# A small input tile moved into the norm constant's place, in a one-core S4D and token-mixer kernel

## The chip, the cores and the metric

The kernel runs on one core of a Trainium2 chip. Its time is the device time of one launch in microseconds (us). The time that is compared is the median of several runs; the profile is of one execution.

A core has a matrix engine (PE, whose weight loads are listed apart as PEld), a vector engine (DVE), a scalar engine (ACT), a general engine (POOL), and a queue (SP) from which nearly all transfers are issued. On-chip memory (SBUF) has 128 partitions; a tile takes the same bytes, at the same place, in each of its partitions.

## What is computed

A block of 2048 tokens by 448 channels goes through two parts, each with a layer norm whose shift, scale and gate come from a conditioning vector `c`:

```python
mod = (_silu(c) @ w_mod).reshape(c.shape[0], 6, 1, -1)
sa, ca, ga, sb, cb, gb = (mod[:, 0], ..., mod[:, 5])
h = _layernorm(x) * (1 + ca) + sa
x = x + ga * _A_ref(h, ...)          # S4D: a long convolution along the tokens
h = _layernorm(x) * (1 + cb) + sb
x = x + gb * _B_ref(h, ...)          # mixer: an MLP along the tokens
```

`_A_ref` builds a convolution kernel of 2048 taps for each of 448 channels out of 256 complex exponentials, and convolves by Fourier transforms of length 4096. `_B_ref` normalizes once more, multiplies by `w1` (2048 to 1792, along the tokens), adds `b1`, takes GELU, multiplies by `w2` (1792 to 2048) and adds `b2`. All is float32.

## The kernel before, in words

**Stages.** The first 56 steps make the convolution kernel, 8 channels at a step: ACT takes exponentials and sines, POOL and DVE multiply them (L656, L679 to L687), PE sums them up (L710). Between them run the first norm, the transform of the input (L553, L581) and, from step 32 on, the products of spectra and the inverse transform for the first half of the channels (L805, L814, L816, L817, L831, L837). After step 56 come the second half of the channels, the return to tokens (L1243 to L1259) and the second norm (`ln_mod`, `ln_out`). The token MLP then has two products. Each is done as three products of a high and a low part: L1373 to L1375 for `w1`, with the normalized tokens `h3h` and `h3l` as the streamed operand, and L1442 to L1444 for `w2`, with `uh` and `ul`. A weight tile is 128 by 896; it is loaded into `w`, and ACT and DVE split it into `whi` (L207) and `wlo` (L216).

**Order.** The order on PE, ACT, DVE and POOL is the one in which the code issues. SP's order is written out by hand at the beginning, up to step 8, and again from the second half of the channels to the end of the first MLP product's normalized rows; between the two the framework's planner orders the transfers.

**Places in SBUF.** Tiles come from pools. A pool takes its place on a stack from below, or, with `side="right"`, on a second stack from above. The pool `cp` is the first of the lower stack and stays to the end. It holds `mod3` to `mod5`, then `eps_t`, `sc`, `ft`, `b1` and `b2`. All other pools of the lower stack lie above it: `y0` (`wm0` and `yk0`, the spectra of the first half), `qp`, `sp2`, `xp` (`xt`, `yt`), `up` (`yi`, `uo`), `fp` (`yk1`, `u`, `si`, `zx`, `zy`, `z`, `vt`), `swp`, and in the MLP `mk` (`h3h`, `h3l`), `mu` (`uh`, `ul`) and `m2r` (`u`, `x2`, `y`). On the upper stack are, among others, the tables `tab`, the exponents' tiles, `mag`, `w` of POOL's products, `E` and `G`, and in the MLP the weights `w`, `whi`, `wlo` (pool `mw`), the rows `xt` that the second norm adds to (pool `mx`) and the pool `mr` of the second norm.

Each tile's bytes are rounded up to a multiple of 32. In the program before, `eps_t` lies at byte 21888 of each partition, `sc` at 21920, `ft` at 21984, `wm0`, `yk0` and later `h3h` at 22368, `h3l` at 51040, `uh` at 79712 and `ul` at 92256.

**The two tiles.** `eps_t` (128 x 1) holds the norm's 1e-5. DVE writes it at L241; ACT reads it at L462 (first norm) and L1230 (second norm, 32 times); at L1332 ACT takes its square root in place, only to have a table loaded, and DVE writes it again at L1333. `sc` is four of the sixteen columns of a 112 x 16 tile: ACT writes exp(-c) there (L913), DVE turns it into silu(c) (L848 to L850) and spreads it out (L851, L508, L509) as the stationary operand of the products with `w_mod`.

Of the kernel before, what the change touches and what calls it, by code (L numbers as in the profile page):

```python
# [11 lines left out]
F32 = mybir.dt.float32  # L12
# [10 lines left out]
P = 128  # L23
# [198 lines left out]
def tile_adaln_s4d_mixer(ctx, tc, i, out):  # L222
# [10 lines left out]

    cp = ctx.enter_context(tc.tile_pool(name="cp", bufs=1))
    mod = [None] * 3 + [cp.tile([P, D], F32, name=f"mod{k}") for k in range(3, 6)]
    eps_t = cp.tile([P, 1], F32, name="eps_t")
    sc = cp.tile([112, 16], F32, name="sc")[:, 0:4]
    ft = cp.tile([P, 64], F32, name="ft")
    b1 = cp.tile([P, 14], F32, name="b1")
    b2 = cp.tile([P, 16], F32, name="b2")  # L240
# [1235 lines left out]
```

## Time and profile before

| | |
|---|---|
| median of 3 runs | 691.31 us (689.89 to 692.56) |
| the profiled execution's own time | 689.93 us |
| its span, first to last instruction | 688.0 us |
| mean granted PE clock in it | 0.969 |

A busy PE is not PE at its peak: matmuls overlap, so the pace is read from the starts of successive matmuls. A row of the groups by line gives line, engine, operation, tiles, shapes and count, then busy time and mean duration, then the engine's idle time just before and who ended it. A row of one tile's or one line's instructions gives a duration as least, median and largest in ns, and the start of the first and the last. A row of the stretches gives the length, then the busy time of each engine with its number of instructions, the granted PE clock, the share of time in which the DMA engines were busy, and what they moved in GB/s.

The span in 40 slices, from the page (one digit is the busy share in tenths, PEclk the granted PE clock):

```profile
PE   0887889879988899999999899999999999999997
PEld 0454445435545566565667667779999999999996
DVE  7599799888779596877967478777322543333331
ACT  5967698888989999999935588877222422222210
POOL 6497467358368888898847000000000000000000
PEclk9998979989999999999999999999999999999999
DMA  7695643568895956353359899946764255555530
```

Slice 1 is 17.2 us long, as all are. POOL's work ends in slice 22, with the convolution; the MLP fills slices 24 to 40.

### The profile page before, as it was taken

The page shows a single profiled execution, that of the slowest core. Times are in us where ns is not written, and L with a number is a line of the kernel's source. Part 1 is how long each engine was busy: PE and PEld are TensorE (multiplying, and loading weights), DVE is VectorE, ACT ScalarE, POOL GpSimd, SP SyncE. Part 2 cuts the span into 40 slices and gives each one's busy share as a digit, 9 for nine tenths or more (in the row PEclk, how much of TensorE's full clock was granted, in tenths as well). Part 3 has the DMA queues.
Part 4 walks back from the last instruction along what each step waited for, and adds up shares of the span by engine and source line. Part 5 has one row for each costly group of instructions (what it writes and reads, how often), then busy time and mean ns, then how long its engine had stood idle before and what let it go on. Part 6 is the DMA issues. An engine that isn't in the chain of part 4 may idle for free. (4 is left out here: it accounts for less than half of the span.)

```text
span 688.0 us, 18263 instructions
## 1 busy us (share of the span) xinstructions
PE 622.3 (90%) x7180; PEld 458.4 (67%) x7180; DVE 452.8 (66%) x870; ACT 438.8 (64%) x880; POOL 268.6 (39%) x323
## 2 busy tenths in 40 slices
PE   0887889879988899999999899999999999999997
PEld 0454445435545566565667667779999999999996
DVE  7599799888779596877967478777322543333331
ACT  5967698888989999999935588877222422222210
POOL 6497467358368888898847000000000000000000
PEclk9998979989999999999999999999999999999999
DMA  7695643568895956353359899946764255555530
GB/s 175 198 196 129 204 161 120 185 212 260 249 298 175 239 134 195 97 152 101 107 158 321 227 251 242 239 123 175 194 190 136 84 163 160 162 161 162 161 114 28
DMA packets 105923, 121.14 MB, mean 176 GB/s; under 512 B 13098, under 2 KB 94286, under 8 KB 105710
## 3 DMA queue, kind: packets, MB, share of 16 engines
q1 hardware_dynamic: 104478, 113.92, 58.1%
q0 software_dynamic: 1360, 6.06, 4.0%
q8 instruction: 57, 0.93, 0.6%
q14 instruction: 28, 0.23, 0.1%
HBM read 84.59 MB, written 34.87 MB: 174 GB/s over the span
## 5 line engine op out<-in xcount | busy, mean ns | idle before, releaser
L207 ACT CAST whi<-w 128x896 fp32r<-128x896 f32 x64 | 59.9, 940 | 139.4 <-PE o L1443 87.1
L679 POOL TENSOR_TENSOR G<-mag,gs 128x512 f32<-128x512 f32 x56 | 71.8, 1282 | 67.4 <-ACT gs L675 67.2
L216 DVE TENSOR_TENSOR wlo<-w,whi 128x896 fp32r<-128x896 f32 x64 | 68.0, 1086 | 41.5 <-ACT whi L207 32.0
L1373 PE MATMUL acc<-h3h,whi 128*128 128x448 f32 x224 | 84.1, 375 | 1.3 <-ACT h3h L1278 1.3
L1374 PE MATMUL acc<-h3l,whi 128*128 128x448 f32 x224 | 82.8, 370 | 0.1
L1375 PE MATMUL acc<-h3h,wlo 128*128 128x448 f32 x224 | 82.4, 368 | 0.0
L1443 PE MATMUL o<-ul,whi 128*128 128x448 f32 x224 | 82.0, 366 | 0.0
L1444 PE MATMUL o<-uh,wlo 128*128 128x448 f32 x224 | 82.0, 366 | 0.0
L1442 PE MATMUL o<-uh,whi 128*128 128x448 f32 x224 | 82.0, 366 | 0.0
L710 PEld LDWEIGHTS kg<-E,G 128*32 128x32 f32 x3584 | 57.4, 116 | 35.5 <-issue 13.9
L627 PE MATMUL xg<-tab,lph 64*128 64x512 f32 x112 | 65.8, 589 | 11.2 <-ACT gs L676 4.6
L710 PE MATMUL kg<-E,G 128*32 128x64 f32 x3584 | 67.3, 230 | 7.8 <-ACT ks L724 3.4
L680 POOL TENSOR_TENSOR G<-mag,gs 128x512 f32<-128x512 f32 x56 | 72.0, 1285 | 0.0
L627 PE MATMUL xe<-tab,lph 64*128 64x512 f32 x112 | 65.8, 589 | 4.4 <-ACT gs L676 2.6
L1446 DVE SCALAR_TENSOR_TENSOR y<-o,b,mod 128x448 f32<-128x448 f32 x16 | 10.9, 684 | 83.1 <-PE o L1444 83.1
L656 POOL TENSOR_TENSOR m<-mag,w 128x512 f32<-128x512 f32 x56 | 59.0, 1054 | 4.4
L681 DVE TENSOR_TENSOR E<-m,xe 128x512 f32<-128x512 f32 x56 | 38.2, 682 | 22.9 <-ACT xe L674 19.1
L1373 PEld LDWEIGHTS acc<-h3h,whi 128*128 128x128 f32 x224 | 42.4, 189 | 14.6 <-ACT h L1283 4.2
L627 PE MATMUL xe<-tab,lex 64*128 64x512 f32 x56 | 31.2, 573 | 18.4 <-POOL dsk L477 17.1
L1374 PEld LDWEIGHTS acc<-h3l,whi 128*128 128x128 f32 x224 | 42.5, 190 | 4.2 <-DVE h3l L1285 0.4
L1375 PEld LDWEIGHTS acc<-h3h,wlo 128*128 128x128 f32 x224 | 42.5, 190 | 3.6
L1443 PEld LDWEIGHTS o<-ul,whi 128*128 128x128 f32 x224 | 42.1, 188 | 3.6
(239 smaller groups left out, 1445.7 us busy)
## 6 DMA issues: line engine op xcount, KB each, us to landing
w<-in_B_w_dram SPq DMA_DIRECT2D x64, 224.0 KB
w<-in_B_w_dram SPq DMA_DIRECT2D x32, 448.0 KB
yu_d<-yt SPq DMA_DIRECT2D x16, 448.0 KB
yi<-yu_d SPq DMA_DIRECT2D x16, 448.0 KB
us_d<-uo SPq DMA_DIRECT2D x16, 448.0 KB
u<-us_d SPq DMA_DIRECT2D x32, 224.0 KB
v_d<-vt SPq DMA_DIRECT2D x32, 224.0 KB
vt<-v_d SPq DMA_DIRECT2D x14, 448.0 KB
```

Source lines behind the costliest of these rows:

```text
L207: self.nc.scalar.copy(hi, w)
L216: eng.tensor_tensor(lo, w, hi.bitcast(F32), ALU.subtract)
L627: T.matmul(out[k], lhs[r], rhs[r], start=start, stop=stop)
L679: G.tensor_tensor(Gt[:, 1], mg_, v32(sg), ALU.mult)
L680: G.tensor_tensor(Gt[:, 0], mg_, v32(cg_), ALU.mult)
L710: T.matmul(kgs[g][32 * q : 32 * q + 32, m], Gt[:, c, d], E[:, c, d], start=h == 0 and c == 0 and m == 0, stop=h == 1 and c == 1, skip_grou ...
L1373: nc.tensor.matmul(acc[f], hi[:, fs], h3h[:, r], start=r == 0, stop=False)
L1374: nc.tensor.matmul(acc[f], hi[:, fs], h3l[:, r], start=False, stop=False)
L1375: nc.tensor.matmul(acc[f], lo[:, fs], h3h[:, r], start=False, stop=r == 15)
L1442: nc.tensor.matmul(o, hi[:, ks], uh[kh][:, k], start=kh == 0 and k == 0, stop=False)
L1443: nc.tensor.matmul(o, hi[:, ks], ul[kh][:, k], start=False, stop=False)
L1444: nc.tensor.matmul(o, lo[:, ks], uh[kh][:, k], start=False, stop=kh == 1 and k == 6)
```

## The change

`eps_t` and `sc` become two parts of one tile of 128 x 5: columns 0 to 3 (partitions 0 to 111) are `sc`, column 4 is `eps_t`. The padding of `sc` from 4 to 16 columns goes. Every later tile on the lower stack starts 64 bytes lower; nothing else is edited.

```diff
     mod = [None] * 3 + [cp.tile([P, D], F32, name=f"mod{k}") for k in range(3, 6)]
-    eps_t = cp.tile([P, 1], F32, name="eps_t")
-    sc = cp.tile([112, 16], F32, name="sc")[:, 0:4]
+    small_t = cp.tile([P, 5], F32, name="small_t")
+    eps_t, sc = small_t[:, 4:5], small_t[0:112, 0:4]
     ft = cp.tile([P, 64], F32, name="ft")
     b1 = cp.tile([P, 14], F32, name="b1")
     b2 = cp.tile([P, 16], F32, name="b2")
```

## The prediction

> **What bounds the kernel now.** I read the stretches first, because the change moves tiles in all stages and each stage has its own limit.
>
> ```profile
> core 0: us, PE busy (x) PEld busy (x) DVE busy (x) ACT busy (x) POOL busy (x), PEclk, DMA share, GB/s
> 150.00:200.00 50.00, 46.84 (x770) 24.36 (x769) 37.81 (x72) 43.50 (x89) 31.49 (x35) 0.96 0.81 243
> 200.00:250.00 50.00, 43.55 (x992) 27.03 (x987) 41.39 (x77) 46.79 (x92) 41.69 (x47) 1.00 0.74 211
> 350.00:370.00 20.00, 19.76 (x207) 13.79 (x197) 13.66 (x24) 9.17 (x39) 11.45 (x20) 1.00 0.83 241
> 370.00:385.00 15.00, 14.34 (x120) 11.06 (x120) 7.51 (x15) 8.67 (x31) 7.03 (x12) 1.00 0.94 301
> 385.00:402.00 17.00, 14.77 (x65) 9.79 (x63) 12.51 (x37) 10.75 (x25) 0.00 (x0) 0.90 0.86 225
> 402.00:465.00 63.00, 63.00 (x296) 48.22 (x295) 49.82 (x149) 51.11 (x113) 0.00 (x0) 1.00 0.89 206
> 465.00:546.00 81.00, 81.00 (x399) 74.58 (x398) 31.92 (x47) 28.70 (x38) 0.00 (x0) 1.00 0.57 165
> 546.00:684.00 138.00, 137.38 (x674) 126.14 (x672) 54.28 (x70) 29.47 (x33) 0.00 (x0) 1.00 0.48 137
> ```
>
> From 402 to 684 us PE never stops: this is the MLP, 282 us or 41% of the 688.0 us span, and it goes at PE's pace. In the earlier stages PE, ACT and POOL are all near full and share the limit. Between 350 and 402 the transfers are densest (0.83 to 0.94 of the DMA engines' time), and there PE stands still for 0.24 + 0.66 + 2.23 = 3.1 us. The list of waits agrees for the MLP: the long ones are waits for PE.
>
> ```profile
> ACT whi L207 <- PE o L1443: 87.1, 27, 3.3
> DVE y L1446 <- PE o L1444: 83.1, 16, 7.2
> ...
> PE xe L627 <- POOL dsk L477: 17.1, 1, 17.1
> ```
>
> The third is PE's wait at the very start, for the first loads and what is made of them.
>
> So a move of tiles can do much only if it alters how fast PE reads its operands; on other engines and on transfers it has a few us at stake at most.
>
> **The change part by part.** *(a) Two tiles become one.* No instruction, no operand size and no transfer is added or taken away. What could come in is a wait, if the order of accesses were kept for the whole tile instead of its two parts. The accesses:
>
> ```profile
> L913 ACT ACTIVATE sc<-cvec x1: 188/188/188, 14.1 to 14.1; 112x4 f32<-112x4 f32 x1
> L850 DVE TENSOR_TENSOR sc<-sc,cvec x1: 161/161/161, 18.2 to 18.2; 112x4 f32<-112x4 f32 x1
> L509 DVE COPY yk<-sc x1: 216/216/216, 239.7 to 239.7; 112x128 f32<-112x128 f32 x1
> ```
>
> ```profile
> L241 DVE MEMSET eps_t<- x1: 59/59/59, 0.8 to 0.8; 128x1 f32 x1
> L462 ACT ACTIVATE rs<-mv,eps_t x1: 308/308/308, 68.2 to 68.2; 128x16 f32<-128x16 f32 x1
> L1332 ACT ACTIVATE eps_t<-eps_t x1: 203/203/203, 384.4 to 384.4; 128x1 f32<-128x1 f32 x1
> ```
>
> In time the two tiles interleave as L241 (0.8 us), L913 (14.1), L850 (18.2), L462 (68.2), L509 (239.7), L1332 (384.4). Each new wait would be for something that ended 13, 50 or 144 us before: L913 for L241, L462 for L850, L1332 for L509. Nothing is late, so nothing queued behind these instructions on ACT is held. What a wait that is already met may still cost is an instruction of its own:
>
> ```profile
> L590 ACTq EVENT_SEMAPHORE  x8: 38/38/38, 162.0 to 207.5; - x8
> ```
>
> Three of 38 ns are 0.1 us. I take 0, and keep 0 to +0.1.
>
> *(b) 64 bytes.* With places in steps of 32 bytes, `eps_t` (4 bytes) and `sc` (64) take 32 + 64 = 96; the new tile (20 bytes) takes 32; the difference is 64, as the change says. A new wait by place needs a lower-stack tile that now touches a tile of the upper stack which it did not touch. Going through the places of all tiles of the program before, one pair does: the buffer of `yt` that starts at byte 120736, where a late buffer of POOL's `m2` ends; after the change they share 64 bytes. The last `yt` store is issued at 138.0 us, and the late `m2` buffers come into use after step 32, around 239 us.
>
> ```profile
> L558 SPq DMA_DIRECT2D yu_d<-yt x16: 512/530/594, 73.3 to 138.0; - x16
> ```
>
> A hundred us lie between; cost 0. All tiles of the lower stack move together and keep their places relative to one another.
>
> *(c) Reading and writing at a new place.* In the MLP the weights `w`, `whi`, `wlo` and the residual rows are on the upper stack and stay; the streamed operands move. `h3h` goes from byte 22368 to 22304. In remainders of 256 that is 96 to 32; of 128, 96 to 32; of 64, 32 to 32. So whatever repeats every 64 bytes or less can't change. A row of 448 floats is 1792 bytes, seven times 256, so all rows have the same remainder, and a row touches 15 blocks of 128 bytes, or 8 of 256, before and after alike. What the trace shows of engines working at places 64 bytes or less apart:
>
> ```profile
> L656 POOL TENSOR_TENSOR m<-mag,w x56: 1047/1050/1187, 19.0 to 316.6; 128x512 f32<-128x512 f32 x56
> ```
>
> ```profile
> L1230 ACT ACTIVATE rs<-ss,eps_t x32: 294/295/296, 388.2 to 467.1; 128x1 f32<-128x1 f32 x32
> ```
>
> `w` of L656 has two buffers of 64 bytes side by side, used in turn: least and median are 3 ns apart over 56 uses. `ss` and `rs` of L1230 go through six buffers with places 32 bytes apart: the 32 durations differ by 2 ns. For places 896 bytes apart (three and a half times 256), POOL's two halves of `z` take
>
> ```profile
> L816 POOL TENSOR_TENSOR z<-zx,zy x27: 657/664/678, 247.1 to 377.4; 128x224 f32<-128x224 f32 x27
> L817 POOL TENSOR_TENSOR z<-zx,zy x27: 657/663/674, 247.8 to 378.1; 128x224 f32<-128x224 f32 x27
> ```
>
> that is, the same. For POOL and ACT I take 0; DVE too, its nearest rows being these. They are a small operand and halves, not a whole MLP row, so PE is bounded for itself:
>
> ```profile
> 599.37 0.36 PE L1442 MATMUL o<-uh,whi 128*128 128x448 f32 x1
> 599.57 0.37 PE L1443 MATMUL o<-ul,whi 128*128 128x448 f32 x1
> 599.78 0.36 PE L1444 MATMUL o<-uh,wlo 128*128 128x448 f32 x1
> 599.98 0.37 PE L1442 MATMUL o<-uh,whi 128*128 128x448 f32 x1
> 600.18 0.37 PE L1443 MATMUL o<-ul,whi 128*128 128x448 f32 x1
> 600.39 0.36 PE L1444 MATMUL o<-uh,wlo 128*128 128x448 f32 x1
> ```
>
> ```profile
> 385.71 3.29 PE L1253 MATMUL y<-vt,fl 128*128 128x224 f32 x16
> ```
>
> ```profile
> L1253 PE MATMUL y<-vt,fl x32: 352/352/457, 378.9 to 388.7; 128*128 128x224 f32 x32
> ```
>
> Five steps take 600.39 - 599.37 = 1.02 us: a matmul of the MLP starts every 0.204 us, with weights in three places and moving rows in two, one step like the next. The quickest pace with as many weights loaded between is L1253's: (3.29 - 0.35) / 15 = 0.196 us. The six MLP lines have 224 matmuls each, 1344 in all. If the 8 ns between the two paces came from the place, the MLP could gain 1344 x 0.008 = 10.8 us; if the new place cost as much again, it could lose 10.8 us. I take 0, as the rows with neighbouring places say, and keep both ends.
>
> *(d) Transfers.* Tiles of the lower stack that transfers read and write: `xt`, `yt`, `yi`, `uo`, `u`, `si`, the `vt` stores, the output. They can be late for PE at the start, where no row moves a load by 64 bytes and I take 0, and between 350 and 402. The most they can give there is PE's 3.1 us; the same 3.1 us is my bound for a loss. I take 0. [...]
>
> **Sum.** Against the profiled execution, 689.93 us (span 688.0): 0 + 0 + 0 + 0, so 689.9. That execution is 1.4 us below the median of the runs shown, 691.31; as the comparison is by medians I predict **691.0 us**. About 0.5%, 3.5 us, is what a measurement of this kernel can tell from no change.
>
> **The rivals.** *PE slows down* (slower). The place is the streamed operand's read in L1373 to L1375 and L1442 to L1444; the mechanism is that a row that starts 32 bytes past a multiple of 128 is fetched later than one that starts 96 past it. The price is up to 8 ns on 1344 matmuls: 691.0 + 10.8 = 701.8. It decides from 3.5 / 1344 = 2.6 ns per matmul. For it: 282 us hang on this one pace, and all streamed rows of the MLP have one remainder, so no row of before compares two. Against it: the L656 and L1230 rows, and the equal count of blocks.
>
> *PE speeds up* (faster). The same place and price the other way: 691.0 - 10.8 = 680.2. For it: L1253 shows that 0.196 is possible. Against it: L1253 streams half the columns and in another form.
>
> [...]
>
> *The change does nothing it says* (the tile rounded up to the old size): 691.3, the same in a measurement.
>
> **Chances.** Forecast, time within 0.5%: 0.60, with the handover at 0.08 and no move at 0.02 beside it; PE slower 0.14; PE faster 0.16. So faster by over 0.5%: 0.16; within: 0.70; slower: 0.14. The forecast's own range is 687.5 to 694.8. To hold 8 in 10 the range reaches some two thirds into the two PE cases: 684 to 698.
>
> **What would show it.** After the change the starts of L1442 to L1444 should still be 0.204 us apart, and those of L1373 to L1375 after 465 us too; 402 to 684 should stay 282 us long; L656, L814 and L1230 should keep their durations to within some ns; the first L1373 should come within 2 us of where it did; no wait should name `sc`, `eps_t` or `yt` anew. A pace other than 0.204 makes the prediction wrong at (c); a shift of the first L1373 by more than 3 us makes it wrong at (d) or in the stages before, where PE, ACT and POOL share the limit and I have no row that moves a whole operand by 64 bytes.

## The result, and the profile after

Over 20 runs of each kernel the median goes from 692.64 to 688.07 us. The ratio is 0.9924, with a 95% interval of 0.9907 to 0.9940: between 4.2 and 6.4 us of 692.64 are saved. (The ratio is not the quotient of the two medians; that is 0.9934, inside the same interval.) The profiled execution took 685.43 us, its span is 683.7.

The stretches of the changed kernel (columns as before: length, busy time of each engine with its number of instructions, granted PE clock, DMA share, GB/s):

```profile
core 0: us, PE busy (x) PEld busy (x) DVE busy (x) ACT busy (x) POOL busy (x), PEclk, DMA share, GB/s
350.00:370.00 20.00, 19.43 (x226) 13.96 (x228) 13.62 (x25) 8.88 (x38) 11.40 (x18) 1.00 0.79 230
370.00:385.00 15.00, 15.00 (x128) 11.45 (x124) 8.10 (x15) 8.41 (x31) 7.69 (x12) 1.00 0.95 299
385.00:402.00 17.00, 14.16 (x64) 9.24 (x62) 11.99 (x38) 11.59 (x27) 0.00 (x0) 0.90 0.87 232
402.00:465.00 63.00, 63.00 (x299) 48.99 (x299) 50.22 (x150) 52.07 (x113) 0.00 (x0) 1.00 0.87 209
465.00:546.00 81.00, 81.00 (x406) 75.92 (x406) 33.45 (x51) 29.47 (x40) 0.00 (x0) 1.00 0.58 165
546.00:684.00 138.00, 132.99 (x665) 124.30 (x664) 53.51 (x67) 28.51 (x31) 0.00 (x0) 1.00 0.49 139
```

Up to 402 us the engines' times differ by under 1 us a stretch. From 402 on PE is still never idle and the clock is still 1.00, but more matmuls fit: 406 instead of 399 between 465 and 546, a stretch of 81 us in both. The last stretch ends early.

The pace of the MLP is read from one line's first and last start. L1442 is every third matmul of the second product; between its first and its last start lie 223 x 3 = 669 steps. A row gives least, median and largest duration in ns, then the first and last start. Before:

```profile
L1442 PE MATMUL o<-uh,whi x224: 358/367/373, 546.1 to 682.6; 128*128 128x448 f32 x112
```

After:

```profile
L1442 PE MATMUL o<-uh,whi x224: 362/362/363, 544.4 to 678.2; 128*128 128x448 f32 x112
```

136.5 / 669 = 0.2040 us a step before, 133.8 / 669 = 0.2000 after. (Starts are rounded to 0.1 us here, so the last digit of a pace is good to 2.) The durations of this line, which spread over 15 ns before, now agree to 1 ns. For all 1344 matmuls of the MLP, 4.0 ns are 5.4 us, 0.78% of 692.64: the whole change, within its interval. The two traces have these 5.4 us: from the first to the last matmul start the MLP takes 290.37 us before and 284.94 after. In the two profiled executions the span differs by 4.3 us; the missing 1.1 us lies ahead of the MLP, whose first matmul starts at 392.64 us before and at 393.69 after. In the traces of the experiments that start lies between 392.39 and 403.16 us.

The rows on which the other zeros stood kept their durations. Of the changed kernel:

```profile
L656 POOL TENSOR_TENSOR m<-mag,w x56: 1046/1048/1188, 18.8 to 318.4; 128x512 f32<-128x512 f32 x56
```

```profile
L1230 ACT ACTIVATE rs<-ss,small_t x32: 294/295/299, 389.2 to 467.0; 128x1 f32<-128x1 f32 x32
L913 ACT ACTIVATE small_t<-cvec x1: 187/187/187, 13.7 to 13.7; 112x4 f32<-112x4 f32 x1
...
L1332 ACT ACTIVATE small_t<-small_t x1: 203/203/203, 385.5 to 385.5; 128x1 f32<-128x1 f32 x1
```

L656 keeps its 1.05 us, L1230 its 295 ns, and no wait names the joint tile anew. DVE's L814 keeps its duration to 2 ns at the median. Before, then after:

```profile
L814 DVE TENSOR_TENSOR zx<-kx,u x32: 610/622/627, 230.9 to 377.2; 128x448 f32<-128x448 f32 x32
```

```profile
L814 DVE TENSOR_TENSOR zx<-kx,u x32: 609/624/626, 232.0 to 378.2; 128x448 f32<-128x448 f32 x32
```

### The profile page after: what moved, and what is told of

The parts are those of the page before. It is cut to its first block, busy times and chain, and to the rows that moved or that the text cites. A ratio compares the mean times of both kernels' runs of the same rounds, so it can differ in the third digit from the quotient of the medians.

```text
span 683.7 us, 18263 instructions
## 1 busy us (share of the span) xinstructions
PE 612.7 (90%) x7180; PEld 456.0 (67%) x7180; DVE 452.6 (66%) x870; ACT 439.0 (64%) x880; POOL 268.1 (39%) x323
## 5 line engine op out<-in xcount | busy, mean ns | idle before, releaser
L1442 PE MATMUL o<-uh,whi 128*128 128x448 f32 x224 | 81.2, 362 | 0.0
L1444 PE MATMUL o<-uh,wlo 128*128 128x448 f32 x224 | 80.6, 360 | 0.0
L627 PE MATMUL xg<-tab,lph 64*128 64x512 f32 x112 | 62.9, 563 | 12.4 <-DVE E L687 4.7
L627 PE MATMUL xe<-tab,lph 64*128 64x512 f32 x112 | 63.5, 569 | 4.7 <-ACT gs L676 2.6
L656 POOL TENSOR_TENSOR m<-mag,w 128x512 f32<-128x512 f32 x56 | 58.9, 1052 | 4.4
L1442 PEld LDWEIGHTS o<-uh,whi 128*128 128x128 f32 x224 | 42.0, 188 | 3.4
```

The costliest lines, as they stand in the source:

```text
L627: T.matmul(out[k], lhs[r], rhs[r], start=start, stop=stop)
L1442: nc.tensor.matmul(o, hi[:, ks], uh[kh][:, k], start=kh == 0 and k == 0, stop=False)
L1444: nc.tensor.matmul(o, lo[:, ks], uh[kh][:, k], start=False, stop=kh == 1 and k == 6)
```

## The experiments

Three theories stood at first. A: the pace hangs on the streamed row's own place. B: it hangs on the distance between the row that PE streams and the weights that it loads meanwhile. C: the new layout of the earlier stages did it, and the MLP's operands have no part. All places and distances below are remainders of 256 bytes; a distance is the streamed row's place less the weights' place. Before the change it is 96 - 224, that is 128; after it 32 - 224, that is 64.

The first tool is a pad in the MLP's own pool. It moves `h3h`, `h3l`, `uh`, `ul` and what lies above them, and nothing that is in use before the MLP. Its filling runs on POOL, which has nothing else left to do by then (in the trace of before POOL runs no instruction from 385 us on). The two added lines push line numbers up by 2:

```diff
         kp = es.enter_context(tc.tile_pool(name="mk", bufs=1))
...
+        pad_t = kp.tile([P, 48], F32, name="pad_t")
+        G.memset(pad_t, 0.0)
         h3h = kp.tile([P, 16, D], F32R, name="h3h")
```

**192 bytes: the changed kernel's place in the MLP alone.**

> The kernel before, with a pad of 192 bytes ahead of h3h only: h3h, h3l, uh, ul come to remainder 32 of 256, as after the change; every earlier tile stays. Theory A (the MLP's pace hangs on the remainder of the streamed row): pace 0.200 us a matmul instead of 0.204, 1344 x 4.0 ns = 5.4 us off, 402 to the end shorter by that, time about 5.4 us below the kernel before. Theory C (the pace hangs on something else that the program's new layout changed, in the earlier stages or in all of it): 0.204, no change of time.

```profile
L1444 PE MATMUL o<-uh,whi x224: 363/363/363, 550.0 to 683.8; 128*128 128x448 f32 x112
```

133.8 / 669 = 0.2000. The median of its 12 runs is 688.87 us against 692.83 for the kernel before; the ratio is 0.9929, interval 0.9895 to 0.9963, which holds the changed kernel's 0.9924 (and the quotient of these medians, 0.9943). C falls: the earlier stages lie where they lay, and the gain is there. In the profiled execution of this kernel the MLP's first matmul starts as late as 399.36 us, with the tiles of the stages ahead of it where they were. One trace of each kernel does not separate spread from cause here; but the 20 runs of the kernel before alone spread from 689.87 to 696.79 us, so the 1.1 us above need no cause in the change.

**64 and 32 bytes.**

> Pad of 64 bytes: the streamed rows come to remainder 160 of 256, that is 32 of 128. Theory A with a period of 128 bytes: pace 0.200. Theory A with a period of 256 or more: another pace than 0.200, 0.204 if two remainders of 256 share it. Theory C: 0.204.

```profile
L1444 PE MATMUL o<-uh,whi x224: 361/361/361, 547.0 to 682.3; 128*128 128x448 f32 x112
```

135.3 / 669 = 0.2022, neither of the two paces. Place 160 is not as good as place 32: the pace does not repeat every 128 bytes.

> Pad of 32 bytes: remainder 128 of 256, a multiple of 64 and of 128. Theory A: if a row that starts on a multiple of 64 or 128 is read best, the pace is below 0.200, down to L1253's 0.189 (1344 x 15 ns = 20 us off); if rows at 32 past a multiple of 64 are as good, 0.200 or 0.204. Theory C: 0.204.

```profile
L1444 PE MATMUL o<-uh,whi x224: 362/362/363, 545.4 to 679.2; 128*128 128x448 f32 x112
```

0.2000. A row that starts at a multiple of 128 is not better than one that starts 32 past it. The single time, 686.69 us, fits.

**The weights moved instead.** A pad above `wlo` in the weights' pool moves `w`, `whi`, `wlo` and the pools below them; the streamed rows stay where they were before the change.

```diff
         lo = self.pool.tile([P, 896], F32R, tag="wlo", name="wlo")
+        if n == 0:
+            pad_w = self.pool.tile([P, 48], F32, tag="pad_w", name="pad_w", bufs=1)
+            self.nc.gpsimd.memset(pad_w, 0.0)
```

> The streamed rows stay at remainder 96 of 256; the weights w, whi, wlo go 192 bytes lower, from remainder 224 to 32, so that the distance from weights to streamed rows is, in remainders of 256, what it is after the change (64). Theory A (the streamed row's own remainder): 0.204, as before. Theory B (the distance between the two operands that PE reads at once): 0.200.

```profile
L1445 PE MATMUL o<-uh,whi x224: 362/362/363, 553.7 to 687.5; 128*128 128x448 f32 x112
```

0.2000, with every streamed row at its old place 96. Theory A falls; this is what B foretold. The single time, 694.93 us, doesn't show the gain: in that execution the MLP's first matmul starts at 403.16 us, 10.5 later than in the profile of before. Whether that is the spread of executions or a price of moving the upper stack this single time can't settle; the next experiment, which moves the same pools by 64 bytes and was timed, shows no such price beyond its interval.

**The changed kernel with its distance undone.** The same pad, of 64 bytes, in the changed kernel: rows at 32, weights at 160, distance 128 again, and neither operand where it was before.

> The changed kernel, with w, whi, wlo 64 bytes lower too: streamed rows at remainder 32 of 256 as after the change, weights at 160; the distance from weights to streamed rows is 128 again, as before the change. Theory B (the distance): 0.204, the change's gain of 5.4 us is undone, time as the kernel before. Theory C2 (each operand's own remainder adds its part): the rows at 32 keep their gain, 0.200 or what the weights at 160 add; 0.204 would be a coincidence.

```profile
L1445 PE MATMUL o<-uh,whi x224: 358/367/373, 550.3 to 686.8; 128*128 128x448 f32 x112
```

136.5 / 669 = 0.2040, and the durations are those of before to the last digit: 358, 367, 373. The ratio to the kernel before is 1.0009, interval 0.9986 to 1.0032: the change's gain is gone, though all of the change is in. By all starts in the two traces, the steps run through the same five lengths too: 196, 200, 203, 209 and 212 ns. Two parts, one for each operand's own place, could still add up to this, but only if the two moves happened to cancel. Two pairs of places with distance 128 (96 and 224, 32 and 160) give 0.2040; two with 64 (32 and 224, 96 and 32), in three kernels, give 0.2000.

**Only `whi` moved.** The pad of 64 bytes between `whi` and `wlo` in the changed kernel gives `whi` distance 128 and leaves `wlo` at 64.

> The changed kernel, with w and whi 64 bytes lower, wlo as after the change: distance 128 for whi, 64 for wlo. Theory B with the weights that are loaded while a row streams: the steps that follow L1442 and L1444 (whi is loaded next in the first and the third of the three products) are long, the one in which wlo is loaded is short; mean between 0.200 and 0.204, about 0.2027. If the distance to the weights in use counts, the same mean with other steps long. If whi does not matter: 0.200.

```profile
L1445 PE MATMUL o<-uh,whi x224: 362/362/363, 546.3 to 681.6; 128*128 128x448 f32 x112
```

135.3 / 669 = 0.2022, in between and a little under the expected 0.2027. Which steps are long was foretold wrongly: by all starts in the trace, the step that follows the first product is 200 ns long, that after the second 204 and that after the third 202.5. This matches neither "the weights being loaded" nor "the weights in use"; which of the two counts stays open. A step may carry over into the next, which no run here tests.

**The other distances.**

> Pad of 160 bytes in the kernel before: streamed rows at remainder 0 of 256, weights at 224, distance 32. Theory A's last form (a row that starts on a multiple of 256 is read best): below 0.200. Theory B: a function of the distance that is 0.200 at 64 and 160 and 0.204 at 128; at 32, away from 128, it should be 0.200 or below.

```profile
L1444 PE MATMUL o<-uh,whi x224: 369/369/369, 549.3 to 687.5; 128*128 128x448 f32 x112
```

138.2 / 669 = 0.2066, the slowest of all, with rows that start at a multiple of 256. The expectation of 0.200 or below was wrong.

> Pad of 128 bytes: streamed rows at remainder 224 of 256, the same as the weights, distance 0. Theory B, if two reads in one and the same part of 256 bytes disturb each other most: above 0.204, so slower than before the change (each 1 ns is 1.3 us). Theory B, if 128 is the worst distance: 0.200. A period of 128 bytes: 0.204.

```profile
L1444 PE MATMUL o<-uh,whi x224: 362/365/369, 544.9 to 680.4; 128*128 128x448 f32 x112
```

0.2025: rows and weights at the same remainder are not the worst.

> Pad of 224 bytes in the kernel before: streamed rows at remainder 64 of 256, weights at 224, distance 96. The distances measured so far: 0 0.2027, 32 0.2067, 64 0.2000, 128 0.2040, 160 0.2000, 192 0.2022. Theory B with the distance as the only input gives no formula; between its neighbours 64 and 128 I expect 0.200 to 0.204. A pace below 0.200 would be a layout better than the changed one; 0.200 would say that this is a floor.

```profile
L1444 PE MATMUL o<-uh,whi x224: 365/367/370, 549.2 to 686.6; 128*128 128x448 f32 x112
```

0.2054, more than either neighbour.

> Pad of 96 bytes: streamed rows at remainder 192, weights at 224, distance 224, the last of the eight. Odd multiples of 32 so far: 32 gives 0.2067, 160 gives 0.2000, 128 apart from each other and 6.7 ns apart, so the period is not 128. Expected between the neighbours 192 (0.2022) and 0 (0.2027); below 0.200 would be a better layout.

```profile
L1444 PE MATMUL o<-uh,whi x224: 363/363/363, 547.6 to 684.4; 128*128 128x448 f32 x112
```

0.2045, also more than either neighbour. Together, from the rows above, and by all starts of the second product in each trace (of several kernels with one distance, all agree):

| distance from weights to streamed row | 0 | 32 | 64 | 96 | 128 | 160 | 192 | 224 |
|---|---|---|---|---|---|---|---|---|
| us a matmul | 0.2025 | 0.2066 | 0.2000 | 0.2054 | 0.2040 | 0.2000 | 0.2022 | 0.2045 |
| by all starts | 0.2027 | 0.2067 | 0.2000 | 0.2053 | 0.2040 | 0.2000 | 0.2022 | 0.2044 |
| kernels | 1 | 1 | 3 | 1 | 2 | 1 | 1 | 1 |

There is no smooth curve, and 0.2000 is the least, at 64 and at 160. The granted clock is 1.00 from 546 to 684 us before, after and with the distance undone (`after_weights64`), and from 465 to 546 us at distance 32 too (394 matmuls there against 406 after the change), so the clock does not make these differences. The four kernels of this part were timed once each, at 695.02, 687.95, 694.10 and 691.88 us; the one with a pad of 64 bytes took 689.79, the one with only `whi` moved 688.88. As single times differ by several us for one and the same kernel, the comparison goes by the pace. The change took the kernel from a middling distance to one of the best; none of these layouts beats it.

**Half the weights.** The last two take the suspected partner away: 64 weight columns instead of 128, except in the first and the last group of each sum. For the groups between, half of the output rows are left out, so these kernels don't compute the whole result. The streamed rows keep their length and place.

```diff
-                    ks = slice(k * P, (k + 1) * P)
-                    nc.tensor.matmul(o, hi[:, ks], uh[kh][:, k], start=kh == 0 and k == 0, stop=False)
...
+                    m = P if 7 * kh + k in (0, 13) else P // 2
+                    ks = slice(k * P, k * P + m)
+                    nc.tensor.matmul(o[0:m], hi[:, ks], uh[kh][:, k], start=kh == 0 and k == 0, stop=False)
...
```

> The same halving at distance 32, where the pace with 128 columns is 0.2067, the worst of the eight. Theory B: the 6.7 ns over distance 64 shrink to half or less, and the pace comes near that of the other halved kernel. If the streamed row or the weights' place matters without the read beside it: still 6.7 ns above the other halved kernel.

Sixteen starts of that kernel, in a stretch of 64-column matmuls (start, duration, engine, line; the first, the second and the last):

```profile
603.88 0.36 PE L1451 MATMUL o<-uh,wlo 128*64 128x448 f32 x1
604.08 0.36 PE L1449 MATMUL o<-uh,whi 128*64 128x448 f32 x1
...
606.88 0.36 PE L1451 MATMUL o<-uh,wlo 128*64 128x448 f32 x1
```

(606.88 - 603.88) / 15 = 0.200: at distance 32, where 128 columns take 0.2066, the whole excess is gone in this stretch.

> The changed kernel (distance 64, pace 0.200), with 64 instead of 128 weight columns in the MLP's matmuls, but for the first and last of each sum; half of the sums are left out, so it is not the reference's output. The streamed rows are as long as before and the weight load reads half as much beside them. Theory B (two reads at once): the pace falls below 0.200, toward 0.187 to 0.190 (448 columns of L1253's kind at half the count per column). If a streamed row alone sets the pace: 0.200.

```profile
603.93 0.36 PE L1449 MATMUL o<-uh,wlo 128*64 128x448 f32 x1
604.13 0.36 PE L1447 MATMUL o<-uh,whi 128*64 128x448 f32 x1
...
606.96 0.36 PE L1449 MATMUL o<-uh,wlo 128*64 128x448 f32 x1
```

3.03 / 15 = 0.202, not below 0.200 as expected, but a little above. The weight loads beside these matmuls, in the kernel before and in the halved kernel at distance 32:

```profile
L1442 PEld LDWEIGHTS o<-uh,whi x224: 187/188/189, 545.9 to 682.4; 128*128 128x128 f32 x112
```

```profile
L1449 PEld LDWEIGHTS o<-uh,whi x224: 134/135/188, 549.6 to 684.0; 128*64 128x64 f32 x96, 128*128 128x128 f32 x16
```

So the part that hangs on the place changes with the number of weight columns: it went at distance 32 and came at distance 64. With loads of 135 ns instead of 188 the step still isn't below 0.200, which speaks against the load's length as what sets the 0.200. That the place works through the load is argued and not shown by these two kernels alone, as fewer weight columns also mean fewer output rows; for it speaks that moving nothing but the upper stack, with the weights on it, changed the pace.

## Why the prediction was right or wrong

The time lies inside the range, 684 to 698, but not with the forecast: a change within 0.5% was given 0.70, and the measured one is 0.76%, at least 0.60% by its interval. What happened is the rival "PE speeds up", which had 0.16. The range held the time because it had been stretched into the two PE cases (to about half way, not the two thirds that the text says), and not because the forecast's account was right; for that account it is luck.

- **(a) Two tiles become one: right.** The joint tile's instructions keep their durations, and the waits are the old ones. The timed kernel that undoes only the distance has both tiles joined and comes out at 1.0009.
- **(b) 64 bytes, and no new wait by place: right** as far as the traces show. No engine waits for `yt` anew.
- **(c) Reading at a new place: right for POOL, ACT and DVE as far as the rows above go, wrong for PE.** This is the step that failed. The text took 0 for PE "as the rows with neighbouring places say". Those rows are of other engines and could not speak for PE's two operands. The six matmuls that it showed all had one distance, 128; the text says itself that no row of before compares two places. They did not step alike either: the starts shown are rounded to 10 ns, and by all starts in the trace of before the steps run through 196, 200, 203, 209 and 212 ns, while after the change each line has one step (202, 201 and 197). Evenness alone is no sign of a good pace, though: at distance 32, the slowest, all steps are 206 or 207 ns. With no row that varied the thing in question, the bounds of 10.8 us on both sides deserved more than 0.30 of the chance. The measured term is 5.4 us, half the bound.
- **The bound itself** came from L1253's 0.196, which is misread: the last of those matmuls takes 457 ns (the largest in its row), not 350, so the pace is (3.29 - 0.457) / 15 = 0.189 us, and by the text's own rule the bound would have been 1344 x 0.015 = 20 us. Either bound was too generous: 0.2000 is the least of the eight distances, and halving the weights doesn't go below it.
- **The rival's mechanism** named the row's own start, 32 or 96 past a multiple of 128. The moved weights show that it is not that alone, and fit the distance: at the same place 96 the pace was 0.2040 with weights at 224 and 0.2000 with weights at 32. The arguments from remainders (the count of blocks touched, nothing can change that repeats every 64 bytes) looked at one operand and were beside the point.
- **(d) Transfers: 0, not contradicted.** With 5.4 us for the MLP, an interval of 4.2 to 6.4 leaves between -1.2 and +1.0 us for everything else. The 0.08 for a quicker handover was the author's guess, and no run shows one: PE stands still for 3.1 us between 350 and 402 us before and for 3.4 after, and between 345 and 386 us the 896-byte packets, those of the `v_d` stores and others, took 41 ns at the median in both traces.

## What to carry to other kernels

When PE never idles and full weights are loaded beside the matmuls, as here, its pace can hang on where the two operands lie to each other (here 0.2000 to 0.2066 us a matmul): try a pad of 32 to 224 bytes ahead of one of them and read the pace from the first and last start of one line. A pad in the stage's own pool tells such an effect from everything else that a layout change does. Evidence for "no effect of the place" has to come from rows in which the place in question differs; rows that all share it say nothing, and then both bounds are real cases. Starts rounded to 10 ns can hide steps that differ by 16 (196 to 212 ns before the change).

## What the runs showed of the hardware that was not expected

In this MLP a matmul that streams 448 columns beside a load of 128 weight columns (188 ns at the median) starts every 0.2000 to 0.2066 us at a granted clock of 1.00, by the two operands' distance in remainders of 256 bytes. 32 bytes can cost 6.6 ns (distance 32 against 64), which over 1344 matmuls would be 8.9 us. The streamed row's own place does not decide it alone: moving the weights without the streamed rows changed the pace from 0.2040 to 0.2000, and halving the weights removed the excess at distance 32 (0.2066, and 0.200 in the stretch shown).

Two other matmul lines (L581, L1253) kept their pace through the change: by the starts in the traces, the most frequent step is 376 ns and 189 ns in both kernels, nearly twice the MLP's time for a column (376 / 448 and 189 / 224 are 0.84 ns, 200.0 / 448 is 0.45). But both operands of each lie on the lower stack and moved together, so their distance stayed, and these rows don't say whether such matmuls depend on it.

Open are why these distances and not others are good, whether and how the two reads disturb each other, whether 256 bytes are the true period (only eight distances were tried, and rows of one tile are 1792 bytes apart at one mean pace), and what sets the 0.2000.
